# Batch 0's attention laid out by token slot, and a new order of work, in a gated attention and channel mixer kernel

## The chip, the cores and the metric

The kernel runs on one core of a Trainium2 chip. The metric is the time of one execution in device microseconds (us). The core has four engines that compute: PE (TensorE, matmuls into the banks of PSUM), DVE (VectorE), ACT (ScalarE) and POOL (GpSimd). SP (SyncE) and ACT each have a queue on which transfers are issued. Every engine works through its own instructions in order and waits on semaphores for the others.

## The reference

```python
B, H, S, D = 4, 8, 768, 48
state = zeros((B, H, D, D))
for t in range(S):
    state = alpha[:, :, t, :, None] * state + einsum('bhd,bhe->bhde', k[:, :, t], v[:, :, t])
    y[:, :, t] = einsum('bhd,bhde->bhe', q[:, :, t], state)
x = y.transpose(0, 2, 1, 3).reshape(B, S, H * D)          # 4, 768, 384
h = maximum(x.transpose(0, 2, 1) @ w_tok1, 0) @ w_tok2    # 768 -> 256 -> 768 over tokens
u = x + h.transpose(0, 2, 1)
out = u + maximum(u @ w_ch1, 0) @ w_ch2                   # 384 -> 1536 -> 384 over channels
```

Inputs and output are float32; the kernel computes its products in bfloat16.

## The kernel before, in words

**Attention blocks.** The recurrence is computed in blocks of 256 tokens: three for each of the four batches, n = 0 to 11. A block lies on 128 partitions with two neighbouring tokens on each partition (the *slots*); partitions 0 to 63 are the first 128 tokens (the first *half*) and 64 to 127 the second. For each block four loads of 384 KB bring alpha, k, q and v (`at`, `kt`, `qt`, `vt`). Blocks 0 to 2 (`WIDE`) take the logarithm of alpha for both slots (`ln`), sum it up along the tokens on PE (`cumw`), and take the exponentials of the sums and of their negatives (`E`, `IE`; `Et` for the totals of the halves). `kk` and `qq` scale keys and queries with these. Both are transposed: on PE (`trk`, `trq`) with an eviction from PSUM (`evk`, `evq`), or by a DMA transpose on SP (`dk`, `dq`, then `pq` to reorder the queries). The other blocks do the same with one sum for a pair of tokens.

`G` forms the products of keys and queries, 16 small matmuls for each half, on tiles of 48 rows by 64 columns of PE; `mask` on DVE drops the products of later keys. `K` forms the key-value product of each half, from which the state after it follows: on DVE `sa` adds the earlier state and `sm`, on DVE or POOL, multiplies with the decay. `y` adds up the masked products with v, `ia` and `ib` add the part of the earlier state, `x` copies the result from PSUM.

Before, `K` and `y` use all 128 rows of PE. For that, each half's two slots must be stacked on the 128 partitions, so copies of half a tile move them: `vs0`, `vs1` for v and `ka`, `kb`, `kc` for the keys (`vswap` and `kturn`).

**Mixer.** For each batch: `t1` (token product into 256, then `ht`), `t2` and `u` (back to tokens, plus x), the transpose of u, then 24 runs `c1` of three matmuls (L811) with a `rt` eviction each, and `c2` (L816) with the last add `o` and the store. The transpose of u goes over PE (`up`, L803, evicted by `ut`) in the batches listed in `UP`, else by two DMA transposes on SP (`ux`). The weights are loaded as float32 in 384 KB pieces (`ldw`) and cast (`cw`).

**Order.** Nothing is scheduled while the kernel is built. `build` names every operation, and `ORDER` is one long written list of these names with a letter for the engine (t PE, s ACT, v DVE, g POOL, y SP); each engine issues its own in that order, and `BUFS` lists the buffer of every value as it is first used. `f3_cumw0t` is a dummy entry: three matmuls of a zero tile with 512 columns, put before `cumw0`. DVE and POOL steps that are marked `port=True` wait for the last such step of the other engine (`shared`). In the list, batch 0's attention stands first, and the attention of a later batch is woven into the mixer of the one before.

Of the kernel before, what the change touches and what calls it, by code (L numbers as in the profile page):

```python
# [96 lines left out]
NB = 3  # L97
NX = 6
KFN = 0
LAST = (3, 0)  # L100
UP = (0, 1)
# [9 lines left out]
WIDE = (0, 1, 2)  # L111

# [3 lines left out]
def build(g):  # L116
# [8 lines left out]
    def filler(nm, bank):  # L125
        return [P.op(f"f{z}_{nm}", {"PE": pe([512] * z)["PE"], "NONE": (0.0, 0.0)}, -100, writes=[bank],
                     emit=lambda e, z=z: g.fill(bank, z)) for z in (1, 3)]

    def attention(n):
# [8 lines left out]
        def fill(nm, bank):  # L138
            return filler(f"{nm}{n}", bank) if n < NB else []

        at, kt, qt, vt = V("in"), V("in"), V("in"), V("in")
        ld = {}
        for v, nm in ((at, "at"), (kt, "kt"), (qt, "qt"), (vt, "vt")):
            ld[nm] = P.op(f"ld_{nm}{n}", {"SP": (420.0, 420.0), "ACT": (374.0, 374.0)}, -90000.0 + 10 * n, writes=[v],
                          emit=lambda e, v=v, nm=nm: g.load(e, nm, v, b, k, ld[nm]), dma=("i", IN_NS, 1500.0, 650.0))
        la, E, IE = V("la"), V("E"), V("IE")
        pkk, pkq, vb = V("pkk"), V("pkq"), V("vb")
        k_in, q_in = [ld["kt"]], [ld["qt"]]
        if n in WIDE:
            lnp = O("ln", act(800, True), 0, writes=[la], reads=[at], preds=[ld["at"]], emit=lambda e: g.lnw(la, at))  # L150
            cb = V("pair")
            cum = O("cumw", pe([384] * 4 + [4] * 8 + [16]), 2, writes=[cb, E, IE], reads=[la], preds=[lnp] + fill("cumw", cb),
                    emit=lambda e: g.cumw(cb, la))
            e1 = O("E", act(768), 4, writes=[E], reads=[cb], preds=[cum], emit=lambda e: g.exps(E, cb, 1.0))
            et = O("Et", act(16), 6, writes=[E], reads=[cb], preds=[cum], emit=lambda e: g.exptot(E, cb))
            e2 = O("IE", act(768), 3, writes=[IE], reads=[cb], preds=[cum], emit=lambda e: g.exps(IE, cb, -1.0))
        else:
# [8 lines left out]
            e1 = et = O("E", act(400), 4, writes=[E], reads=[cb], preds=[cum], emit=lambda e: g.expE(E, cb))  # L166
            e2 = O("IE", act(384), 4, writes=[IE], reads=[cb], preds=[cum], emit=lambda e: g.expIE(IE, cb))
# [5 lines left out]
        kk = O("kk", either(dve(768), pool_tt(768)), 5, writes=[pkk], reads=[kt, IE], port=True, preds=k_in + [e2],  # L173
               emit=lambda e: g.scaled(e, pkk, kt, IE, wide))
        qq = O("qq", either(dve(768), pool_tt(768)), 5, writes=[pkq], reads=[qt, E], port=True, preds=q_in + [e1],
               emit=lambda e: g.scaled(e, pkq, qt, E, wide))
# [3 lines left out]
        if n < NX:  # L180
            bk, bq = V("one"), V("one")
            trk = O("trk", pe([128] * 8), 8, writes=[bk], reads=[pkk], preds=[kk] + fill("trk", bk),
                    emit=lambda e: g.trw(bk, pkk))
            evk = O("evk", either(dve(1024, True), act(1024)), 9, writes=[tpk], reads=[bk], preds=[trk],
                    emit=lambda e: g.trwev(e, tpk, bk))
            trq = O("trq", pe([128] * 8), 8, writes=[bq], reads=[pkq], preds=[qq] + fill("trq", bq),
                    emit=lambda e: g.trw(bq, pkq))
            evq = O("evq", either(dve(1024 * 1.065), act(1024 * 1.34)), 9, writes=[tpq], reads=[bq], preds=[trq],
                    emit=lambda e: g.qev(e, tpq, g.bank(bq).bitcast(BF16)))
        else:  # L190
            evk = O("dk", {"SP": (1240.0, 1240.0)}, 9, writes=[tpk], reads=[pkk], preds=[kk],
                    emit=lambda e: g.xbar(tpk, pkk), dma=("x", 1400.0, 1180.0, 480.0))
            tqx = V("tpk")
            xq = O("dq", {"SP": (1240.0, 1240.0)}, 9, writes=[tqx], reads=[pkq], preds=[qq],
                   emit=lambda e: g.xbar(tqx, pkq), dma=("x", 1400.0, 1180.0, 480.0))
            evq = O("pq", either(dve(1024), act(1024 * 1.35, True), {"POOL": (1100.0, 1140.0)}), 9.5, port=True, writes=[tpq], reads=[tqx], preds=[xq],
                    emit=lambda e: g.qev(e, tpq, g.t(tqx)))
        gtm = V("gtm")
        masks = []
        for hf in range(2):  # L200
            gp = V("pair")
            G = O(f"G{hf}_", pe([128] * 4), 10 + hf, writes=[gp], reads=[tpk, tpq], preds=[evk, evq] + fill(f"G{hf}", gp),
                  emit=lambda e, hf=hf, gp=gp: g.gmm(gp, tpk, tpq, hf), mode="G")
            masks.append(O(f"mask{hf}_", dve(1024), 12 + hf, writes=[gtm], reads=[gp], preds=[G],
                           emit=lambda e, hf=hf, gp=gp: g.mask(gtm, gp, hf)))
        nst = 2 if k < NB - 1 else 1
        kp = V("pair")
# [4 lines left out]
        vsw = lambda hf, preds: shift(f"vs{hf}_", 10, [vb], [vt], preds, lambda e: g.vswap(e, vb, vt, hf))  # L212
        turned = n >= KFN
        if turned:
            vs = [vsw(hf, [vc]) for hf in range(2)]
            kx, kp_in = None, [kk, vc, vs[0]]
            if nst == 2:
                kx = V("kt")
                ka = shift("ka", 9, [kx], [pkk], [kk], lambda e: g.kturn(e, kx, pkk, 0))
                kb = shift("kb", 9, [kx], [pkk], [kk], lambda e: g.kturn(e, kx, pkk, 1))  # L220
                kp_in += [ka, kb, vs[1]]
            kc = shift("kc", 9, [pkk], [], [kk, trk if n < NX else evk] + ([ka] if nst == 2 else []),
# [4 lines left out]
        else:  # L227
            KO = O("K", {"PE": (276.0 if nst == 2 else 140.0, 420.0)}, 9.5, writes=[kp], reads=[pkk, vb],
                   preds=[kk, vc] + fill("K", kp) + ([prev_s[1]] if prev_s and k > 0 and n > NB else []),
                   emit=lambda e: g.kmm(kp, pkk, vb, nst), mode="G")  # L230
            vs = [vsw(hf, [KO, vc]) for hf in range(2)]
        before = prev_s if k > 0 else None
        states = [before]
        for hf in range(nst):
            s_, sp = V("ss"), states[-1]
            if sp is None:
                so = O(f"s{hf}_", dve(384), 10, writes=[s_], reads=[kp, E], preds=[KO, et],
                       emit=lambda e, s_=s_, hf=hf: g.sfirst(s_, kp, E, hf, wide, turned))
            else:
                t_ = V("tmp")  # L240
                ad = O(f"sa{hf}_", dve(384), 10 + hf, writes=[t_], reads=[kp, sp[0]], preds=[KO, sp[1]],
                       emit=lambda e, t_=t_, hf=hf, s0=sp[0]: g.sadd(t_, kp, s0, hf, turned))
                so = O(f"sm{hf}_", either(dve(384), pool_tt(384)), 11 + hf, writes=[s_], reads=[t_, E], port=True,
                       preds=[ad, et], emit=lambda e, s_=s_, t_=t_, hf=hf: g.smul(e, s_, t_, E, hf, wide))
            states.append((s_, so))
        for hf, st in enumerate(states[:2]):
            yp, x = V("one"), V("x")
            held = []
            if st:
                held.append(O(f"i{'ab'[hf]}", pe([96] * 4), 13, writes=[yp], reads=[tpq, st[0]],  # L250
                              preds=[evq, st[1]] + (fill("y", yp) if hf else []),
                              emit=lambda e, hf=hf, st=st, yp=yp: g.inter(yp, tpq, st[0], hf)))
            yo = O(f"y{hf}_", pe([48] * 8), 14, writes=[yp], reads=[gtm, vb],
                   preds=[masks[hf], vs[hf]] + held,
                   emit=lambda e, hf=hf, yp=yp, st=st: g.ymm(yp, gtm, vb, hf, not st))
            xo = O(f"x{hf}_", either(act(384), dve(384)), 16, writes=[x], reads=[yp], preds=[yo],
                   emit=lambda e, x=x, yp=yp: g.xev(e, x, yp))
            xs[(b, 2 * k + hf)] = (x, xo)
# [5 lines left out]
    def weight(nm, piece, prio, work=1100.0):  # L264
        raw = V("in")
        o = P.op(f"ldw_{nm}{piece}", {"SP": (420.0, 420.0), "ACT": (374.0, 374.0)}, prio, writes=[raw],
# [4 lines left out]
    def mixer(b):  # L271
# [44 lines left out]
        for mc in range(NDC):  # L316
            rt = V("rt")
            ro = []
            for half in range(2):
                bank = V("one")  # L320
                o = P.op(f"c1_{b}_{mc}_{half}", pe([384] * 3), m0 + (4900 + 975 * mc + 487 * half) * sc, writes=[bank],
                         reads=[ut], preds=(uts[0:2 + half] if b in UP else [uts[half]]) + [wl[("wc1", mc // 6 * 3 + p)] for p in range(3)],
# [34 lines left out]
    for b in range(B):  # L357
        mixer(b)
    return P
# [4 lines left out]
ld_at1s ld_at0y ld_qt0y ld_vt0y ld_kt0s ld_at2y f1_cumw0t ln0s f3_cumw0t f1_trk1t f1_cumw1t f1_trk0t f3_cumw1t  # L364
f1_trq0t f3_trq0t ln1s ld_qt1y f1_trq1t cumw0t cumw1t E0s ld_at3y f3_trk1t IE0s Et0s qq0v vb0s ld_kt1y kk0v trq0t E1s
f3_cumw2t vs1_0g ld_vt1y evq0v trk0t ka0s vs0_0g f1_cumw2t evk0s ld_kt3y qq1v kb0s IE1s f1_G00t G0_0t P3g ld_qt2y
f3_trq1t mask0_0v ln2s Et1s trq1t kc0g ld_vt3y K0t f1_G10t kk1v evq1s G1_0t s0_0v ld_vt2y vb1g trk1t ln13s sa1_0v
# [507 lines left out]
```

## Time and profile before

| | before |
|---|---|
| runs, median (lowest to highest) | 166.52 us (166.51 to 167.97) |
| span of the profiled execution, first to last instruction | 165.0 us |
| own time of the profiled execution | not listed beside its span; the three runs above stand for it |
| PE busy | 156.2 us, 95% of the span |
| DVE, ACT, POOL busy | 121.2, 96.2, 68.7 us |
| HBM read, written | 25.17 MB, 4.72 MB |
| granted TensorE clock | 1.000 |

The span runs from the first to the last instruction of one profiled execution; a run's time also holds what lies around it. Busy times are sums over an engine's instructions. PE's matmuls are pipelined, so that a busy PE is not one at its peak. Line numbers such as L811 are those of the kernel above.

### The profile page before, as it was taken

To read this page: it belongs to the slowest core of one execution; us is meant where nothing else is said; L and a number is where in the kernel's file an instruction comes from. 1 tells how busy PE (TensorE), PEld (TensorE's weight loads), DVE (VectorE), ACT (ScalarE), POOL (GpSimd) and SP (SyncE) were. 2 spreads that over 40 slices of the span, in tenths; PEclk is the share of its full clock that TensorE was granted. 3 is DMA by queue.
4 is the path that set the end of the run, shared out by engine and by line. 5 is a ranking of instruction groups with operands and counts; after the bars stand their busy time and mean duration, and the time that the engine had idled before them with its cause. 6 is when DMAs were issued, how large, how long until landed. Compare 5 with 4: busy or idle time off the path is not lost.

```text
span 165.0 us, 4235 instructions
## 1 busy us (share of the span) xinstructions
PE 156.2 (95%) x1683; PEld 99.2 (60%) x1683; DVE 121.2 (73%) x210; ACT 96.2 (58%) x186; POOL 68.7 (42%) x84
## 2 busy tenths in 40 slices
PE   7969769999999999999999999999999999999992
PEld 2435446666666766576666666666666656656662
DVE  4098989989898898798878999989492455524422
ACT  3599987998877837939887746913614001514110
POOL 4025659497217475792388528973300000000000
PEclk9999999999999999999999999999999999999999
DMA  4999999999999999999989996898001136200213
GB/s 121 324 325 325 337 347 316 365 327 352 371 335 347 326 315 226 307 252 264 136 198 255 211 250 120 219 181 183 0 4 48 49 75 157 105 0 0 99 72 119
DMA packets 74531, 34.48 MB, mean 209 GB/s; under 512 B 67984, under 2 KB 73488, under 8 KB 74512
## 3 DMA queue, kind: packets, MB, share of 16 engines
q1 hardware_dynamic: 50576, 23.30, 55.2%
q10 hardware_dynamic: 23936, 10.91, 24.3%
q8 instruction: 13, 0.21, 0.5%
q14 instruction: 6, 0.05, 0.1%
HBM read 25.17 MB, written 4.72 MB: 181 GB/s over the span
## 4 chain that ended last, share of the span: by engine, by line
PE 83%; DMA 4%; SPq 3%; POOL 2%; issue 2%; ACT 2%; DVE 1%; POOLq 0%; DVEq 0%
PE ps L816 29%; PE ps L811 29%; PE ps L593 14%; PE ps L792 5%; DMA in<-in_v_dram 4%; PE ps L787 4%; SPq L534 3%; PE ps L654 1%; PE ps L803 1%; POOL pkk L642 1%; DVE gtm L700 1%; POOL vb L685 1%; ACT x L684 1%; POOL ss L753 1%; ACT E L626 0%
## 5 line engine op out<-in xcount | busy, mean ns | idle before, releaser
L816 PE MATMUL ps<-wc,rt 128*128 128x384 bf16 (+1 forms) x300 | 54.7, 320 | 0.0
L811 PE MATMUL ps<-ut,wc 128*128 128x384 bf16 x288 | 51.3, 326 | 0.0
L782 ACT ACTIVATE rt<-ps 128x384 bf16<-128x384 f32 x54 | 24.4, 490 | 35.4 <-PE ps L811 34.7
L811 PEld LDWEIGHTS <-wc 128*128 128x128 bf16 x288 | 27.1, 98 | 16.7
L816 PEld LDWEIGHTS <-rt 128*128 128x128 bf16 x300 | 27.5, 98 | 15.9
L700 DVE TENSOR_TENSOR gtm<-ps,mk 128x1024 bf16<-128x1024 f32 x24 | 28.7, 1219 | 4.8 <-PE ps L593 3.4
L784 DVE TENSOR_SCALAR rt<-ps 128x384 bf16<-128x384 f32 x42 | 21.7, 551 | 9.2 <-PE ps L811 9.2
L820 DVE TENSOR_TENSOR o<-ps,u 128x384 f32<-128x384 f32 (+1 forms) x25 | 13.1, 537 | 10.0 <-PE ps L816 9.1
L685 POOL CAST vb<-in 64x384 bf16<-64x384 f32 (+1 forms) x18 | 10.9, 608 | 15.2 <-DVE pkk L642 8.9
L593 PE MATMUL ps<-zs 128*128 128x512 bf16 x38 | 12.7, 452 | 2.9 <-DVE zs L496 1.1
L684 ACT CAST x<-ps 128x384 bf16<-128x384 f32 x17 | 7.8, 477 | 10.7 <-PE ps L593 10.5
L796 DVE TENSOR_TENSOR u<-ps,x 128x384 bf16<-128x384 f32 x24 | 11.8, 550 | 3.0 <-PE ps L792 3.0
L642 DVE TENSOR_TENSOR pkq<-in,E 128x768 bf16<-128x768 f32 x8 | 7.6, 954 | 5.4 <-ACT E L626 5.2
L787 PE MATMUL ps<-x,wt 128*128 128x384 bf16 x48 | 11.1, 325 | 0.5 <-DVE gtm L700 0.4
L684 ACT CAST vb<-in 64x384 bf16<-64x384 f32 (+1 forms) x18 | 11.1, 618 | 0.7 <-DMA in<-in_v_dram 0.2
L642 POOL TENSOR_TENSOR pkk<-in,IE 128x768 bf16<-128x768 f32 x5 | 9.1, 1816 | 4.9 <-DVE pkk L685 3.2
L753 POOL TENSOR_TENSOR ss<-tmp,E 128x384 bf16<-128x384 f32 x11 | 9.2, 833 | 3.2 <-DVE tmp L750 2.9
L750 DVE TENSOR_TENSOR tmp<-ps,ss 128x384 f32<-128x384 f32 x16 | 8.8, 552 | 1.0 <-PE ps L593 0.5
L792 PE MATMUL ps<-ht,wt 128*128 128x384 bf16 x48 | 9.5, 326 | 0.0
L593 PEld LDWEIGHTS <-gtm 128*128 128x128 bf16 x192 | 7.4, 96 | 2.7 <-DVE gtm L700 0.9
L593 PEld LDWEIGHTS <-tpk 48*64 48x64 bf16 x384 | 6.1, 106 | 4.9 <-issue 4.3
L593 PE MATMUL ps<-vb,gtm 128*128 128x48 bf16 x192 | 8.6, 183 | 0.4 <-DVE gtm L700 0.4
(91 smaller groups left out, 216.6 us busy)
## 6 DMA issues: line engine op xcount, KB each, us to landing
in<-in_moe_w_ch_dram SPq DMA_DIRECT2D x10, 384.0 KB, 6.2
in<-in_alpha_dram SPq DMA_DIRECT2D x9, 384.0 KB, 6.8
out_dram<-o SPq DMA_DIRECT2D x16, 192.0 KB, 2.5
in<-in_q_dram SPq DMA_DIRECT2D x7, 384.0 KB, 6.3
in<-in_v_dram ACTq DMA_DIRECT2D x7, 384.0 KB, 6.0
in<-in_k_dram ACTq DMA_DIRECT2D x6, 384.0 KB, 5.7
in<-in_k_dram SPq DMA_DIRECT2D x6, 384.0 KB, 6.2
in<-in_v_dram SPq DMA_DIRECT2D x5, 384.0 KB, 7.2
```

The source lines that it names most:

```text
L593: return self.pe.matmul(out, lhsT=lhsT, rhs=rhs, start=start, stop=stop, skip_group_check=True)
L642: self.shared(self.eng[e].tensor_tensor(self.t(dst)[:, :, :, 0:D], self.t(src).rearrange("p h s d -> p s h d"), bass.AP(tensor=f.tensor, o ...
L684: return self.act.copy(d, s)
L685: return self.shared(self.eng[e].tensor_copy(d, s))
L700: self.nc.vector.tensor_tensor(self.t(gtm)[:, hf, :, :], self.pair(gp).rearrange("p a (j t) -> p (a j) t", t=128), bass.AP(tensor=m.tensor ...
L782: self.act.activation(d, s, AF.Relu)
L784: self.nc.vector.tensor_scalar_max(d, s, 0.0)
L787: self.pe.matmul(self.bank(bank)[:, 0:HD], lhsT=self.wt1[:, kc, m * 128 : m * 128 + 128], rhs=self.t(x), start=(kc == 0), stop=(kc == NS - 1))
L792: self.pe.matmul(self.bank(bank)[:, 0:HD], lhsT=self.wt2[:, kc, i * 128 : i * 128 + 128], rhs=self.t(hts[kc]), start=(kc == 0), stop=(kc = ...
L811: self.pe.matmul(self.bank(bank)[:, 0:HD], lhsT=self.wc1[:, kc, mc * 128 : mc * 128 + 128], rhs=self.t(ut)[:, 3 * half : 3 * half + 3, kc, ...
L816: self.pe.matmul(self.bank(bank)[:, 0 : cz - ca], lhsT=self.t(rts[mc][0])[:, i * 128 : i * 128 + 128], rhs=self.wc2[:, mc, ca:cz], start=( ...
L820: self.nc.vector.tensor_tensor(self.t(o)[:, ca:cz], self.bank(bank)[:, 0 : cz - ca], self.t(u)[:, i % 3, ca:cz], ALU.add)
```

## The change

- Blocks 0 to 2 keep the slots as they are: `G` is split by slot instead of by half (`gslot`, with the new mask table `mkw`), and `K` and `y` run on tiles of 64 rows, one for each half, both halves in one run (`khalf`, `yslot`). The half-tile copies of these blocks are gone. The earlier state is added on PE with an identity matmul (`kadd`, named `A`), and one DVE product with the decay (`sfirst`) makes the new state.
- `Et` is joined to `E`: the totals lie behind the sums in both banks.
- Block 5's keys and batch 1's u are transposed by DMA instead of on PE (`KX`, `QX`, `UP`).
- All loads are issued on SP. The stores are on both queues: 19 on ACT and 6 on SP, where it was 8 and 17.
- The first half of `w_ch1` is loaded in thirds of its columns, each with all its rows, so that a third serves two of the twelve column blocks.
- `ORDER` and `BUFS` are new throughout. The dummy matmuls are 28 instead of 38, and all stand in batch 0's attention.

```diff
-NX = 6
+KX = (5, 6, 7, 8, 9, 10, 11)
+QX = (6, 7, 8, 9, 10, 11)
-UP = (0, 1)
+UP = (0,)
+LOADQ = ({"SP": (420.0, 420.0)}, {"SP": (420.0, 420.0)})
...
+        if wide:
+            kps = [V("one") for _ in range(nst)]
+            K = O("K", {"PE": (350.0, 530.0)}, 9.5, writes=kps, reads=[pkk, vb], preds=kk + [vc],
+                  emit=lambda e, first=before is None: g.khalf(kps, pkk, vb, first), mode="Y")
+            for hf in range(nst):
+                kp, s_, sp = kps[hf], V("ss"), states[-1]
+                KO = K
+                if sp is not None:
+                    KO = O(f"A{hf}_", pe([384]), 9.6 + hf, writes=[kp], reads=[sp[0]], preds=[K, sp[1]],
+                           emit=lambda e, kp=kp, s0=sp[0]: g.kadd(kp, s0))
+                so = O(f"s{hf}_", dve(384), 10 + hf, writes=[s_], reads=[kp, E], preds=[KO, et],
+                       emit=lambda e, s_=s_, kp=kp, hf=hf: g.sfirst(s_, kp, E, hf, wide))
+                states.append((s_, so))
...
+    def gslot(self, gp, tpk, tpq, sl):
+        tk, tq = self.t(tpk), self.t(tpq)
+        for j in range(4):
+            for hf in range(2):
+                for r in range(2):
+                    pr = slice(r * 64, r * 64 + D)
+                    self.mm(self.bank(gp, r)[hf * 64 : hf * 64 + 64, j * 128 : j * 128 + 128],
+                            tk[pr, (sl * 4 + j) * 128 + hf * 64 : (sl * 4 + j) * 128 + hf * 64 + 64],
+                            tq[pr, j * 256 + hf * 128 : j * 256 + hf * 128 + 128], True, True)
+
+    def maskslot(self, gtm, gp, sl):
+        m = self.mkw[:, 1 - sl : 129 - sl]
...
+    def khalf(self, kps, pkk, vb, first):
+        kk, vv = self.t(pkk), self.t(vb)
+        for j in range(4):
+            for sl in range(2):
+                for hf, kp in enumerate(kps):
+                    ph = slice(hf * 64, hf * 64 + 64)
+                    self.mm(self.bank(kp)[:, 96 * j : 96 * j + 96], kk[ph, sl, 2 * j : 2 * j + 2, :],
+                            vv[ph, sl, 2 * j : 2 * j + 2, :], j == 0 and sl == 0, (first and hf == 0) and sl == 1)
+
+    def kadd(self, kp, s0):
+        self.mm(self.bank(kp)[:, 0:HD], self.idn, self.t(s0), False, True)
+
+    def yslot(self, yps, gtm, vb, first):
+        gg, vv = self.t(gtm), self.t(vb)
+        for h in range(H):
+            for sl in range(2):
+                for hf in range(2):
+                    ph = slice(hf * 64, hf * 64 + 64)
+                    self.mm(self.bank(yps[hf])[:, h * D : h * D + D], gg[ph, sl, 4 * (h % 2) + h // 2, :],
+                            vv[ph, sl, h, :], first[hf] and h == 0 and sl == 0, h == H - 1 and sl == 1)
...
 ORDER = """
+ld_at0y ln0s f8_cumw0t f1_cumw0t cumw0t IE0s ld_at1y ln1s ld_kt0y kk0g ld_qt0y E0s qq0v ld_vt0y ld_qt1y vb0v ld_at2y
+ld_kt1y f6_cumw1t f1_cumw1t cumw1t E1s ld_at3y trk0t qq1v evk0v IE1s ld_vt1y ld_at4y ld_kt2y kk1g ln2s ld_qt2y ld_kt3y
+ld_vt2y P3g f1_trq0t trq0t evq0s K0t s0_0v ldw_wt10y ld_vt3y ln13s ld_qt3y f4_cumw2t f1_cumw2t cumw2t vb1g ldw_wt11y
+G1_0t E2s mask1_0v A1_0t ldw_wt20y ldw_wt21y ld_at5y ldw_wc13y r13s ldw_wc15y ldw_wc14y ld_kt4y s1_0v G0_0t trq1t
...
+t2_1_0t o_0_5v ld_kt7y u_1_0v c2_0_4_2t t2_1_2t u_1_2v t2_1_3t t2_1_1t u_1_1v t2_1_4t vs0_6s u_1_4v u_1_3v P7g
+c2_0_0_0t lnP7s st_0_5s c2_0_4_3t ka6g ld_at8y ln18s P8g o_0_4v c2_0_2_2t kb6s c2_0_2_3t st_0_4s o_0_2v t2_1_5t dk6y
+c2_0_0_1t u_1_5v cum7t kc6s k0a7v c2_0_0_2t ld_qt7y vs1_6s K6t c2_0_0_3t IE7s kk7v lnP8s cum8t E7s ux_1_0y c1_1_3_0t
...
```

399 lines of the change are left out of this document (212 added, 187 removed), and 22 rows, old and new, of the table BUFS.

## The prediction

> **What bounds the kernel now.** I read the windows first, cut where the chain of waits changes its kind, then the chain itself, then who waited for whom.
>
> ```profile
> 0.00:31.39 31.39, 25.74 (x339) 15.16 (x340) 22.98 (x44) 24.49 (x41) 14.88 (x29) 1.00 1.04 305
> 31.39:37.34 5.95, 5.95 (x90) 4.29 (x90) 5.34 (x11) 5.56 (x10) 5.66 (x7) 1.00 1.10 338
> 37.34:162.00 124.66, 124.55 (x1257) 79.74 (x1254) 92.54 (x156) 66.12 (x137) 48.14 (x49) 1.00 0.73 180
> ```
>
> First number after the window: its length; then PE, weight loads, DVE, ACT, POOL busy. From 31.39 us on PE never waits. Before, it is idle for 31.39 - 25.74 = 5.65 us, and much of its busy time there is the dummy matmuls (38 of 512 columns). So time can come from two places only: an earlier end of the head (batch 0's attention, first token matmuls), or less PE work after it.
>
> ```profile
> 14.06 7.23 DMA in<-in_v_dram
> ...
> 23.31 1.83 POOL pkk L642
> ...
> 31.39 0.86 PE ps L787 x4
> ...
> 32.99 2.06 PE ps L792 x12
> 35.05 0.17 PE ps L593 x4
> 35.22 0.77 PE ps L803 x12
> 35.99 1.07 PE ps L593 x38
> 37.06 0.44 PE ps L803 x6
> 37.51 2.48 PE ps L811 x15
> ```
>
> The chain in order of time (start, length, what). The head hangs on loads until 21.29, then on batch 0's third block, then PE alone counts. L811, the first channel matmul, begins at 37.34: the milestone of my sum. After it come 124.66 us of PE and 3.0 us of last add and store.
>
> **The sum's base.** The profiled span is 165.0; the runs have a median of 166.52. No own time of the profiled run is given, so I take 1.5 us to lie around the span.
>
> **The head, part by part.** (1) All loads on SP. From 8 to 16 us ACT issued one load, and the core still moved 325 to 327 GB/s, so one queue suffices: 384 KB at 325 GB/s is 1.21 us. The two first alphas share the engines and are used at 5.00; alone, the first lands at about 3.8, the n-th at 3.8 + 1.21(n - 1). Position gives: vt2 (15th) 20.7, wc14 (25th) 32.8. Check: the page's first eight slices hold 25.8 loads' bytes by 33 us. Before, the cast of vt2 began at 23.65. 24 load issues of about 0.38 us leave ACT; 19 instead of 8 stores come to it, off the path where PE never waits. A second mask table costs DVE a fill and four small copies at the start, where it waits 5.19 us for the first E.
>
> (2) Token slots. For three blocks, 13 half-tile copies (0.50 to 0.51 each, 6.6 us of ACT, POOL, DVE) and three small exponentials (0.18) go. Four state steps change from add plus product (0.56 + 0.83 on DVE and POOL) to a 384-column identity matmul (0.16) and one DVE product (0.55): 0.68 less on the chain each time. PE gets: cumulative sums three 16-column matmuls more; key-value products 40 on 64-row tiles for 20 (8 of 96 columns took 0.34; the new runs lie between 0.35, side by side, and 0.68); y 32 for 16 per block. Eight y take 0.20 in the chain, so 32 cost between 0.32 (two tiles at once) and 0.80 (25 ns each); I take 0.45, nearest the 16 G tiles (0.35, 22 ns each). At the dear end PE has 1.6 us more, covered by the 5.65 idle; without that cover it would be paid.
>
> Row first: after a G run on tiles the next three L811 take 0.59 instead of 0.49, so changing tiles costs 0.10. The Trainium skill, TensorEngine Tiling (Array Packing), Tiling Modes, speaks against this change: switching the mode drains TensorE. Six runs more are 0.6 us by it, in the head beside waits; the sum is the same by row and rule.
>
> (3) Dummy matmuls: 28 for 38. The first eleven come every 0.43 us until 5.7, later ones at 0.21, so nine end at 4.9, and the first cumulative sum, begun at 4.9 instead of 6.6, runs partly slow (+0.6). Its input is there at 4.6.
>
> (4) The head walked by hand in the new order, each engine in its own sequence, durations from the rows of before, some 0.05 for each hand-over. Block 0: ln 3.8 to 4.6, sums on PE to 6.1, then ACT does IE, the ln of block 1 and E (0.81 each) to 8.6; kk takes 1.82 on POOL from 7.1 to 8.9, and only then qq 0.96 on DVE to 9.9, since DVE and POOL take turns at the steps marked as sharing a port. ACT is now the long engine: E and IE of block 1, ln of block 2 and block 0's query eviction (1.30) end at 13.1. Block 1: kk waits for its load and ends at 14.4; ACT ends the key eviction at 17.7. Block 2: after a mask (1.22) and a state (0.55) of the earlier blocks DVE does kk and qq from 18.6 to 20.5; ACT evicts the queries to 22.6; after G, DVE has a mask, a state and a mask, to 26.5; y and the x copies end at 28.0. The last token-1 matmul ends at 28.7, ht at 29.9. For the second token product wt21 (21st, 28.0) must be cast too: POOL ends that at 29.6. DVE has four steps of batch 1's first block in between and does the six u of 0.55 from 30.5 to 33.8 (before: 33.49 to 36.37); ut 0.55 to 34.4. The 25th load, 32.8, plus a 0.82 cast behind two other POOL steps gives 34.6. So L811 begins at **34.6**, 2.75 earlier. Bounds: not before 32.8 + 0.6 = 33.4 (gain 3.9); gain 0 if chains slip. The loads already stand right behind the attention: that is what is late next.
>
> **PE work after the milestone.** Batch 1's 18 transposes of u leave PE (0.67 + 0.34 in the chain), and block 5's eight of k (0.45); one inter product of 0.17 moves behind. Net -1.3 us. Four evictions go with them. Their work becomes three DMA transposes on SP (ut row: 1.28 each). On SP ux waits behind dk6 and the load of qt7, and behind it stand dq6 and the loads of block 8.
>
> ```profile
> L668 SPq DMA_TRANSPOSE ut<-u x4: 1242/1280/1307, 104.3 to 136.7; - x4
> DMA to landing us min/median/max: 3.2/3.2/3.9
> ```
>
> These are the transposes of u for batches 2 and 3 (ns of the issue; us to landing). In the new order batch 1 has between the third u's matmul and the first L811 seven c2 runs of 0.49, two t2 of 0.33, two cumulative sums and one K: 4.8 us of PE. Less about 1.0 for u on DVE, 3.8 stand against 3.2 to 3.9. For batches 2 and 3 the same count gives 3.75 and 3.9, less 0.75: 3.0 and 3.15. I allow **1.2 us** of new PE waits; from nothing to 6.6, the longest wait of an SP transpose before:
>
> ```profile
> SPq L664 <- POOL in L578: 6.6, 1, 6.6
> ```
>
> On the same queue dk5, new, waits for POOL's kk of block 5, and behind it stand vt5, at6 and three wc2 pieces; these are wanted after 24 c1 runs (11.7 us), so a hold of a few us is covered; beyond that it would be paid in full.
>
> The wc1 weights in thirds of columns change nothing: wc12 (27th, lands 35.3) is needed after eight c1 runs, 34.6 + 3.9; wc11 (30th, 38.9) after thirteen, 41. Without that lead each late piece would cost 1.21.
>
> The end of the last batch has the same final half add and store, but two 192 KB stores just ahead: 0 to 0.5, I take 0.1.
>
> **Sum.** -2.75 (head) - 1.3 (PE work) + 1.2 (waits) + 0.1 = -2.75. 166.52 - 2.75 = **163.8**; its own range: 166.52 - 3.9 - 1.3 = 161.3 to 164.8.
>
> **Rivals.**
> A: the head does not move. For it: ACT and DVE are busy 24.49 and 22.98 of 31.39 us, so an in-order slip of any chain delays all, and six state, mask and u steps stay. Against: vt2 comes 3 us sooner, 6.6 us of copies go. Then -1.3 + 1.2 + 0.1: 166.5.
> B: slower. SP's single queue is the place: in batch 1 a transpose or load ahead of ux waits as the 6.6 us row did. Waiting t beyond the spare 0.0 to 0.6 us stops PE for t, since everything behind is L811 of the same batch. 6.6 replaces the 1.2: 166.52 - 2.75 - 1.2 + 6.6 = 169.2. It decides the sign from t = 4.0. For: 64 loads, 19 transposes and 6 stores in one line, and one 384 KB load issue took up to 2.98 us under back-pressure. Against: the wait list of PE after 31.4 us is empty with sixteen transposes already on SP; 64 loads need 77 us of the some 100 until the last block.
> C: the new order fits fully: no new waits and L811 held by the loads alone: 161.3.
> D: the slots do not do what they say: K and y run one tile after the other at the dear end and no cover is left in the head: 163.8 + 1.6 = 165.4.
>
> **Chances.** Forecast 0.50; C 0.13; A 0.13; B 0.13; D 0.11. A measurement of this kernel can tell about 1% (1.7 us; the runs span 1.46) from no change. Faster by over 1%, below 164.85: forecast and C, and a fourth of A and D together, 0.69; within 1%: the rest of A and D, 0.18; slower: 0.13. The range 161.0 to 168.0 leaves out most of B (0.11) and the best of C (0.05). The likeliest case's own is 161.3 to 164.8.
>
> **What would show it.** First L811 near 34.6, the first ln begun at 3.8 instead of 5.00, no half-tile copies in the first 25 us; the PE idle after the milestone 1 to 1.5 us and released by DMA ut; PE's work after the milestone near 123.3. Wrong: L811 later than 36, or a single PE wait over 3 us on ut or on a load.

## The result and the profile after

The change makes the kernel slower: 172.07 us (median of four runs, 170.97 to 173.1) against 166.6 us, a ratio of 1.030 with an interval from 1.024 to 1.037. The forecast was 163.8 us, and its range ended at 168.0. The profiled execution took 173.1 us, with a span of 171.4. The mean granted clock of the four executions was 0.98, 0.99, 1.00 and 0.986 (at 173.1, 172.5, 170.97 and 171.65 us): stretches of 3.4 us at half clock, told below, are part of the loss, but the execution at full clock is still 4.4 us above 166.6. Medians here are of all executions of a version, while a ratio and its interval leave out those that took over 1.5% longer than the fastest of their kernel, and set the others against the executions of the kernel before that were on record by then (4 to 19, with medians of 166.6 to 167.25 us).

The windows of the changed kernel, cut where its head ends (columns as before; the first channel matmul, now L890, first runs at 36.43, and without a break from 36.88):

```profile
0.00:31.00 31.00, 26.46 (x406) 16.41 (x407) 19.51 (x44) 20.91 (x30) 15.01 (x25) 0.94 1.01 283
31.00:36.88 5.88, 5.67 (x87) 3.82 (x86) 5.75 (x12) 5.41 (x10) 3.48 (x4) 1.00 1.09 366
36.88:168.04 131.16, 124.92 (x1231) 78.69 (x1231) 87.31 (x145) 69.81 (x141) 52.24 (x53) 0.99 0.76 182
```

Three things differ from the rows of before. The head ends 0.5 to 0.9 us earlier, not 2.75. After it PE is idle for 131.16 - 124.92 = 6.24 us, where it never waited. And the last-but-two column, the granted clock of PE, is 0.94 and 0.99 where it was 1.00. Who stops PE after the head, and what stops DVE (waits: us in total, times, longest):

```profile
PE ps L646 <- DVE u L875: 2.6, 1, 2.6
PE ps L646 <- DVE o L899: 2.3, 2, 2.1
PE ps L646 <- DMA tpk<-pkk: 1.3, 2, 1.0
...
DVE o L899 <- DMA out_dram<-o: 6.6, 4, 2.8
```

The first three rows make up the 6.2 us. No row names `ut`, the releaser that the forecast had named. The row to read is the last: the final add `o` (L899) waits for *stores* of earlier `o` tiles. The chain shows how this reaches PE (start, length, what):

```profile
67.29 4.52 DMA out_dram<-o
...
71.94 0.10 DVE o L899
...
72.41 0.56 DVE u L875
...
73.11 0.33 PE ps L646 x4
```

`o` has three buffers. The new order puts four last adds of batch 0 within 8 us (64.2 to 71.9), but the written list `BUFS` gives them two buffers only: o_0_1 and o_0_4 the first, o_0_5 and o_0_2 the second. So the fourth add, o_0_2, waits 2.78 us for the store of o_0_5, while the third buffer is not in use. That store landed 4.5 us after its issue, and it was issued 2.05 us after its add had ended (65.24), because ACT first stood waiting for POOL:

```profile
67.23 0.52 ACT L637 ACTIVATE la<-in 128x384 bf16<-128x384 f32 x1 [1.51 <-POOL in L631]
67.29 0.34 ACTq L627 DMA_DIRECT2D out_dram<-o  x1
```

u_1_5 stands behind o_0_2 in DVE's line, and PE's K6 stands behind u_1_5, for whose bank it waits. PE's stop of 2.1 us at 97.98 is of the same kind: o_1_2 waits for the first buffer, into which o_0_3 was added by 79.4 and whose store ACT issued only at 92.97; the third buffer had been free since its store landed at 87.2. In the kernel before, stores landed as late (3.5 to 5.4 us), but its list of waits has no such row. What follows the first stop is a second loss (PE alone: length, busy time, granted clock, DMA share, GB/s):

```profile
70.19:73.60 3.41, 0.84 (x11) 1.00 1.23 214
73.60:77.00 3.40, 3.40 (x17) 0.50 1.27 147
```

After a stretch of 3.41 us in which PE worked 0.84, the next 3.41 us run at half clock: 1.7 us of work lost. A like pair stands in the head: 2.03 us busy of 3.41 up to 25.80, then half clock to 29.21. The Trainium skill, TensorE: Matmul & The Clock Gate, Part 1, says that the clock falls to half after an idle window of about 3.4 us. The length agrees; the trace shows that the window need not be wholly idle. Nor does the busy time alone decide: the two half-clock stretches begin 47.8 us apart, 14 times 3.41, and in another stretch of this spacing, 94.09 to 97.50, PE was busy for 1.79 us only and the clock stayed full to 100.9.

The profiled span, against the forecast's own sum (span about 162.3):

| | forecast | measured | difference |
|---|---|---|---|
| end of the head (L890 without a break) | 34.6 | 36.88 | +2.3 |
| PE work after it, at full clock | 123.3 | 124.92 - 1.7 = 123.2 | 0 |
| PE idle after it | 0.1 + 1.2 | 6.24 | +4.9 |
| half clock after the head | 0 | 1.7 | +1.7 |
| last add and store | 3.1 | 3.4 | +0.3 |

### The profile page after: what moved, and what is told of

It reads as the page before. It is cut to its first block, busy times and chain, and to the rows that moved or that the text cites. A ratio compares the mean times of both kernels' runs of the same rounds, so it can differ in the third digit from the quotient of the medians.

```text
span 171.4 us, 4289 instructions
## 1 busy us (share of the span) xinstructions
PE 157.0 (92%) x1722; PEld 98.9 (58%) x1722; DVE 112.9 (66%) x200; ACT 96.1 (56%) x179; POOL 70.7 (41%) x82
## 4 chain that ended last, share of the span: by engine, by line
PE 56%; DMA 21%; SPq 7%; POOL 6%; DVE 4%; issue 3%; ACT 1%; DVEq 0%; POOLq 0%
PE ps L890 24%; PE ps L895 18%; PE ps L646 9%; DMA in<-in_q_dram 7%; DMA in<-in_moe_w_ch_dram 5%; DMA tpk<-pkk 4%; SPq L581 4%; DMA in<-in_alpha_dram 3%; DMA out_dram<-o 3%; PE ps L866 2%; DVE u L875 2%; PE ps L712 1%; POOL in L692 1%; PE ps L871 1%; POOL in L696 1%
## 5 line engine op out<-in xcount | busy, mean ns | idle before, releaser
L890 PE MATMUL ps<-ut,wc 128*128 128x384 bf16 x288 | 53.3, 332 | 0.2
L890 PEld LDWEIGHTS <-wc 128*128 128x128 bf16 x288 | 27.1, 99 | 18.0 <-issue 1.4
L863 DVE TENSOR_SCALAR rt<-ps 128x384 bf16<-128x384 f32 x39 | 20.5, 549 | 9.9 <-PE ps L890 8.8
L758 DVE TENSOR_TENSOR gtm<-ps,mk 128x1024 bf16<-128x1024 f32 x18 | 21.4, 1217 | 4.0 <-PE ps L646 2.4
L899 DVE TENSOR_TENSOR o<-ps,u 128x384 f32<-128x384 f32 (+1 forms) x25 | 13.2, 537 | 15.9 <-PE ps L895 8.2
L700 POOL TENSOR_TENSOR pkk<-in,IE 128x768 bf16<-128x768 f32 x9 | 16.4, 1817 | 11.2 <-ACT IE L687 4.4
L646 PE MATMUL ps<-tpq,tpk 48*64 48x128 bf16 x384 | 8.1, 219 | 3.9 <-DVE o L899 2.1
L646 PE MATMUL ps<-rt 128*128 128x512 bf16 x28 | 9.3, 460 | 1.1 <-DVE rt L538 1.1
L832 POOL TENSOR_TENSOR ss<-tmp,E 128x384 bf16<-128x384 f32 x8 | 6.7, 833 | 8.0 <-DVE tmp L829 5.2
L692 POOL TENSOR_TENSOR in<-in,in 128x384 f32<-128x384 f32 x6 | 6.0, 994 | 7.3 <-DVE gtm L774 3.4
L743 POOL CAST vb<-in 64x384 bf16<-64x384 f32 (+1 forms) x11 | 6.8, 619 | 4.9 <-DVE ss L832 4.2
L696 POOL TENSOR_TENSOR in<-in,lf 128x384 f32<-128x384 f32 x6 | 6.0, 999 | 6.6 <-DVE pkk L700 5.7
```

Source lines behind the costliest of these rows:

```text
L646: return self.pe.matmul(out, lhsT=lhsT, rhs=rhs, start=start, stop=stop, skip_group_check=True)
L700: self.shared(self.eng[e].tensor_tensor(self.t(dst)[:, :, h0:h1, 0:D], self.t(src)[:, h0:h1].rearrange("p h s d -> p s h d"), bass.AP(tens ...
L758: self.nc.vector.tensor_tensor(self.t(gtm)[:, hf, :, :], self.pair(gp).rearrange("p a (j t) -> p (a j) t", t=128), bass.AP(tensor=m.tensor ...
L863: self.nc.vector.tensor_scalar_max(d, s, 0.0)
L890: self.pe.matmul(self.bank(bank)[:, 0:HD], lhsT=self.wc1[:, kc, mc * 128 : mc * 128 + 128], rhs=self.t(ut)[:, 3 * half : 3 * half + 3, kc, ...
L899: self.nc.vector.tensor_tensor(self.t(o)[:, ca:cz], self.bank(bank)[:, 0 : cz - ca], self.t(u)[:, i % 3, ca:cz], ALU.add)
```

## The experiments

Where numbers of buffers change, every class named gets its buffers anew, the one that has been free longest first; line numbers shift with each edit. Each version has one profiled execution. In the eight whose loads up to there are the same (the change itself, 1, 2, 6, 9, 10, 11 and 13) the head ends, without a break, between 36.09 and 37.50 us, and the last piece of w_ch1 that it needs begins its cast between 35.25 and 36.37, so a difference of less than 1 us between two heads says little.

**1. Room for the stores** (`o` six buffers).

```diff
-    "rt": 20, "o": 3,
+    "rt": 17, "o": 6,
```

> The changed kernel with six buffers for the last add (o) instead of three; to make room rt has 17 instead of 20. Theory one (each store lands 4 to 5 us after its issue while loads run, four last adds come within 8 us, so DVE's o waits for a buffer, the u behind it comes late and PE waits for a bank): the DVE waits on stores (6.6 us in four) fall under 0.5, the PE waits of 2.6 and 2.1 us go, and with the first the half-speed window at 73.6 us; 172.1 falls by 4.5 to 6.5, to 165.6 to 167.6. Theory two (SP's one line of loads, transposes and stores makes the transposes late): the PE waits only change their releaser to tpk or ut, and the time stays above 170.5.

Measured: 169.34 us, ratio 1.015 (1.011 to 1.019). DVE's row for `out_dram<-o` falls from 6.6 to 0.4 us, and the half clock after the head is gone; PE's idle time there falls from 6.24 to 4.02 us. That mends 2.7 us, half of the loss, and less than the 4.5 to 6.5 of theory one. The edit changes two things, the number of `o` buffers and which add gets which: it shows what the waits for stores cost, and not that three buffers are too few. No run keeps three and uses the third. The waits that are left:

```profile
PE ps L658 <- POOL tpq L755: 1.6, 2, 1.2
PE ps L902 <- DMA ut<-u: 1.4, 2, 1.0
PE ps L902 <- DVE rt L875: 0.7, 1, 0.7
```

**2. Eight dummy matmuls in the head's idle places.**

```diff
-G0_2t        -K2t        -t1_0_1_0t
+g1_G0_2t G0_2t   +g3_K2t K2t   +g4_t1_0_1_0t t1_0_1_0t
```

> The changed kernel with eight more dummy matmuls (1.7 us) at three places between 22 and 26 us where PE waits in the head: one before the first G of block 2, three before its K, four before the first t1. Theory one (the half-speed window of 25.8 to 29.2 us follows from PE's idle time before it, and holds up the head's end): no half-speed window in the head, first L811 1 to 1.7 us earlier than 36.9, time 0.8 to 1.7 us lower. Theory two (the head's end is set by the landing of the last wc1 piece at 35.95): the window goes, but L811 still begins at 36.6 to 37.0 and the time stays within 0.6 us.

Measured: 171.28 us, 1.027 (1.020 to 1.033). No half clock in the head any more (a stretch came at 94.9 us instead, after 1.23 us of work in 3.41). The head ends at 36.09 without a break instead of 36.88, 0.8 us earlier, and the time falls by as much, between the two theories; the last piece of w_ch1 is cast from 35.25 instead of 36.00. The store waits are all there (6.5 us on DVE).

**3. The slots alone, first try**: the order, queues and pieces of w_ch1 of before, batch 0's attention by slots.

```diff
-KX = (5, 6, 7, 8, 9, 10, 11); UP = (0,); ORDER: new
+KX = (6, 7, 8, 9, 10, 11);    UP = (0, 1); ORDER: of before, with the slots' steps
```

> The kernel before with batch 0 by token slot alone: its order, queues, w_ch1 pieces and PE transposes, with the half-tile copies, Et and the second product of the state left out of the list, the two y of a block as one run at the place of the later one. Theory one (the slots shorten the head): first L811 0.3 to 1.0 us before 37.34, time 165.6 to 166.3. Theory two (tile changes and doubled small matmuls cost as much): 166.6 to 167.3. In either, not the 172.1 of the whole change.

Measured: 170.78 us, 1.026 (1.021 to 1.031), the first channel matmul at 42.7. No theory had that. It is confounded: I had given one product a bank in which it waited for a mask (1.6 us), and the head had two stretches at half clock.

**4. The loads alone**: the kernel before, its 24 loads on ACT issued on SP instead.

```diff
-ld_at1s ld_kt0s ... ld_vt10s
+ld_at1y ld_kt0y ... ld_vt10y
```

> The kernel before with its 24 ACT loads issued on SP at the same places of the list, nothing else. Theory one (one queue carries all loads as fast; the prediction's step): 166.6, within 0.8. Theory two (a load that waits for its buffer holds every later load, transpose and store): loads land later, PE waits appear after 31 us, 168 to 171.

Measured: 169.65 us, 1.012 (1.007 to 1.016). This is theory two. The head is no worse (37.0, with 300 GB/s over its first 37 us against 309), so the forecast's reading that one queue feeds the DMA engines holds; but a line in order lets a load that waits for its buffer hold all behind it. In the profiled execution, one of the longer ones (170.66 us):

```profile
SPq L534 <- DVE wc L685: 3.4, 1, 3.4
```

```profile
PE ps L816 <- ACT wc L684: 2.3, 1, 2.3
```

The first row is SP: a load of v waits for a buffer until DVE has cast the piece of w_ch2 in it, and behind it in the line stands the load of another piece of w_ch2. The second is PE, waiting for that piece. A stretch at half clock follows (62.4 us), and these 2.3 and 1.7 us are the whole difference of the spans (169.0 against 165.0). The Trainium skill, DMA: Bandwidth & Descriptors, Issuing engines are not separate DMA queues, says that issuing on several engines saves only issue time. By bandwidth the trace agrees; the loss comes from what waits behind a waiting load. That the other executions, 1.2% above the kernel before, lose at the same place is likely, but they have no profile.

**5. More load buffers** for the changed kernel.

```diff
-    "in": 19, "rt": 20,
+    "in": 22, "rt": 14,
```

> The changed kernel with 22 load buffers (in) for its 19, paid for with 14 rt buffers for its 20; o stays at 3, order and queues are as they are. Theory one (waits for load buffers in SP's single line hold the head): SP's waits in the first 31 us for a load buffer to come free (1.5 us for the buffer of vb2, and the 1 to 3 us behind POOL and ACT) go, wc14 lands at 33 to 34.8 instead of 35.95, the first channel matmul starts at 34.0 to 35.8 instead of 36.4, and the time falls by 1 to 2.5 us from the changed kernel's 172.1, to 169.6 to 171.1; the o stores' waits (6.6 us on VectorE) stay. Theory two (the rate of the loads themselves sets the head): wc14 lands within 0.5 us of 35.95 and the time stays at 171.5 to 172.5.

Measured: 171.25 us, 1.022 (1.014 to 1.030). The chain of the head:

```profile
27.40 7.54 DMA in<-in_moe_w_ch_dram
...
34.98 0.84 POOL wc L755
...
35.87 2.94 PE ps L902 x17
```

wc14 lands 1.0 us earlier than in the changed kernel (34.94 against 35.95), and the head ends at 35.87 instead of 36.88. Both lie just below the spread of the eight heads told above, so SP's waits for buffers cost something, between 0.2 and 1.6 us at the end of the head; the time falls by 0.8.

**6. Edits 1 and 2 together.**

> The two earlier edits together: 6 o buffers (17 rt), and 8 dummy matmuls ahead of the head's idle places (one before G0_2, three before K2, four before t1_0_1_0). Theory one (the two losses are separate and add up): -2.7 us for the store waits and -0.8 to -1.7 us for the half-speed window in the head, so 167.6 to 168.8. Theory two (the loads set the end of the head, and the half-speed window there lies under the loads' time): the same as with 6 o buffers alone, 169.0 to 169.8.

Measured: 168.83 us, 1.011 (1.006 to 1.016), with 11, which cannot be told from it, the best version of the change that computes the whole result. Its mean granted clock is 0.997. Compare the row after the head with those of before and after:

```profile
36.87:163.88 127.01, 123.42 (x1232) 78.52 (x1232) 87.74 (x145) 70.23 (x141) 52.40 (x54) 1.00 0.76 189
```

PE works 1.1 us less than before (124.55), and is idle 3.6 us.

**7. The slots alone, second try**: as 3, with y1 right after ia1, y0 in a free bank, and twelve dummy matmuls ahead of trq2, ia1, trk3, ia2 and K2.

> Before's order, queues, w_ch1 pieces and TensorE transposes, with batch 0's attention by slots alone, as in the run of slots alone before, but y1 placed right after ia1, y0 in bank 3 so that no product waits for a bank, and 12 dummy matmuls in the gaps the smaller work leaves. Theory one (the slots themselves save time, and what was lost was the stale order): the first channel matmul starts no later than 37.4, there is no half-speed window in the head, and the time is 165.5 to 167.0. Theory two (the slots cost as they stand: less work on TensorE, the same chain through VectorE and ScalarE, loads that end at the same time): the first channel matmul starts at 37.4 to 40 and the time is 167 to 169.5. Above that: the slots' smaller tiles have a cost of their own that I have not named.

Measured: 170.01 us, 1.018 (1.012 to 1.023), above both theories. The clock is full throughout, and after the head PE is idle 0.05 us, as before. All of the loss lies in the head, which ends at 40.9:

```profile
40.90:165.48 124.58, 124.53 (x1257) 79.74 (x1254) 92.39 (x156) 66.08 (x137) 48.24 (x49) 1.00 0.70 175
```

```profile
27.25 3.58 PE ps L661 x69
...
30.86 0.56 DVE ss L840
31.42 1.14 DVE gtm L789
...
32.60 0.65 PE ps L881 x3
```

The chain runs PE (of whose 3.58 us six dummy matmuls take 1.47), a state on DVE, then the two masks of block 2 one after the other on DVE (31.34 to 33.68), for which PE waits. Without the half-tile copies, this head is 3.5 us longer. So in an order made for halves the slots bring nothing; whatever the new kernel's head gains, it gains together with its order.

**8. Buffers, dummy matmuls and vt7 earlier** (five `o`, 21 `in`, 14 `rt`).

```diff
-ld_kt7y ... ld_qt7y ... dq7y ... ld_vt7y dk8y
+ld_kt7y ... ld_qt7y ld_vt7y ... dq7y ... dk8y
```

> The changed kernel with 5 o buffers, 21 load buffers, 14 rt buffers, the 8 dummy matmuls of the head, and the load of vt7 moved up in SP's line from behind the transposes of dq7 to right behind qt7. Theory one (the order of buffers and of SP's line is what was wrong, not the slots): 166 to 168, at or a little above the kernel before; a head that ends at 34.5 to 36, no wait of o for a store over 0.5 us, and the chain no longer through vt7 at 80 us. Theory two (the single line of loads costs by itself, wherever a buffer waits): 168.3 to 169.8.

Measured: 172.09 us, 1.027 (1.018 to 1.037): as slow as the change itself, and neither theory. PE has a new wait behind the head:

```profile
PE ps L911 <- DMA ut<-u: 3.2, 1, 3.2
```

The first transpose of u of batch 1 is issued at 65.90, 1.8 us behind the load of vt7, and lands 7.7 us later, where the two of the changed kernel took 4.9 and 5.9. A stretch at half clock follows at 72.9. Why the transpose took so long is not shown; that it shared the engines with vt7 would fit.

**9 and 10. Loads back on ACT**: 17 loads, in the changed kernel (9) and in the version of experiment 6 (10), at their places in the order.

```diff
-ld_at7y ld_vt7y ld_qt6y ... ld_vt10y ldw_wc24y ldw_wc25y
+ld_at7s ld_vt7s ld_qt6s ... ld_vt10s ldw_wc24s ldw_wc25s
```

> The changed kernel with 17 of its loads (the ones of batches 1 to 3 that the kernel before issues on ScalarE, and two pieces of w_ch2) moved from SP's line to ScalarE's, at their places in the order; nothing else. Theory one (the single line of loads is a loss of its own, apart from the store waits): after the head no wait of TensorE for a load or a transpose of more than 1 us in batch 1, and 1 to 2.5 us less than the changed kernel's 172.1, so 169.6 to 171.1. Theory two (the line costs nothing by itself; only what waits for o and the half-speed windows count): 171.6 to 172.6, or more, since ScalarE issues 17 loads of 0.4 to 0.9 us.

> The run with 6 o buffers and the 8 dummy matmuls (168.8 us) with the same 17 loads on ScalarE's line. Theory one (the rest of the loss, 3.5 us of TensorE waits in batches 1 and 2, comes from loads behind waiting transposes in SP's line): the chain no longer passes through vt7 at 79.8 us, those waits fall below 1.5 us, and the time is 166.0 to 167.4, level with the kernel before. Theory two (the waits come from the order on VectorE and GpSimd, and the loads are just late in it): 168.3 to 169.3.

Measured: 177.46 us, 1.050 (1.040 to 1.061), and 173.05 us, 1.034 (1.026 to 1.041). My theory fell: by the ratios, two lines of loads are worse by about 2% in this order, some 3.4 and 3.8 us. The clock in 10 is full. Two waits of 10 after the head, ACT's and SP's:

```profile
ACT rt L879 <- PE ps L908: 7.7, 8, 1.9
...
SPq L740 <- POOL pkq L718: 10.1, 3, 7.3
```

ACT reaches each load only when its evictions are done, and they wait for PE, as long as in version 6 (7.4 us) but now with loads behind them; and SP, no longer held by its loads, stands at the transposes, once for 7.3 us. The chain still passes vt7, now landing at 86.8 instead of 84.7. That the places in the list were right for one engine only is my reading of this; no run moves the loads to better places on ACT.

**11. The transposes of u on ACT** (version 6).

```diff
-ux_1_0y ux_1_1y ux_2_0y ux_2_1y
+ux_1_0s ux_1_1s ux_2_0s ux_2_1s
```

> The same run (6 o buffers, 8 dummy matmuls, 168.8 us) with the loads left on SP's line and the four transposes of u of batches 1 and 2 (ux) on ScalarE's. Theory one (ux is late because it stands behind waiting loads and transposes in SP's line): the 1.0 us wait for ut goes, loads behind ux come 1 to 2 us earlier, and the time is 167.6 to 168.5. Theory two (ux waits for u itself, or the path lies elsewhere): 168.6 to 169.4.

Measured: 169.29 us, 1.009 (1.004 to 1.014): no difference from version 6, and the wait for `ut` stays (1.0 us there, 0.9 here). What stands in SP's line ahead of `ux` does not hold it: in version 6 SP itself waits there for u.

```profile
SPq L744 <- DVE u L893: 3.3, 2, 2.2
```

**12. All of it**: six `o`, 21 `in`, 13 `rt`, dummy matmuls, and the 17 loads on ACT.

> 6 o buffers, 21 load buffers, 13 rt buffers, the 8 dummy matmuls, and the 17 loads on ScalarE's line: the changed kernel with each known loss mended. Theory one (the slots save what I summed, some 1.3 us of TensorE's work and up to 1 us of the head, once nothing waits): 165.0 to 166.3, faster than the kernel before. Theory two (13 rt buffers or the order bring waits of their own, and the head has no more to give): 166.7 to 168.5.

Measured: 175.22 us, 1.051 (1.043 to 1.060). Neither theory. It is 1.7% slower than 10, so the numbers of buffers (21 `in`, 13 `rt`, dealt out anew) cost as well as the loads on ACT; which of them does is not separated.

**13. vt7 right ahead of dk7** (version 6).

```diff
-ld_at9y ... dk7y ... dq7y ... ld_vt7y dk8y
+ld_at9y ld_vt7y ... dk7y ... dq7y ... dk8y
```

> The run with 6 o buffers and the 8 dummy matmuls (168.8 us), with the load of vt7 moved in SP's line from behind the transposes dk7 and dq7 to right ahead of dk7. Theory one (what is left of the loss in batch 1 is the place of vt7 in the order: GpSimd's cast of it at 84.8 us holds all that is queued behind it): that cast starts at 80 to 82, the 1.1 us wait for tpq at 106 goes, and the time is 167.0 to 168.2. Theory two (the three waits come from the batch's order on VectorE and GpSimd as a whole; another wait takes the place): 168.4 to 169.4.

Measured: 171.59 us, 1.024 (1.019 to 1.030). The wait for `tpq` shrinks to 0.4, and another takes its place. The same wait of PE in version 6, and then here:

```profile
PE ps L908 <- DVE rt L881: 1.4, 1, 1.4
```

```profile
PE ps L911 <- DVE rt L884: 3.1, 1, 3.1
```

What SP waited for between 70 and 86 us tells why:

```profile
SPq L602 <- POOL pkq L721: 2.6, 1, 2.6
```

The moved load keeps the buffer that the list gave it, and this buffer comes free only when a query step on POOL is done. So vt7 issues at 77.90, 1.9 us before its old time (79.81), and dk7, now behind it, at 78.32 instead of 75.06; the transposed keys land at 82.7, the steps of block 7 follow, and `rt` stands behind them on DVE. Here, as in experiment 8, moving one entry of the list moved the loss.

**14. One load fewer ahead of wc14** (version 6).

```diff
-ld_at5y ldw_wc13y ... ldw_wc15y ldw_wc14y
+ldw_wc13y ... ldw_wc15y ldw_wc14y ld_at5y
```

> The run with 6 o buffers and the 8 dummy matmuls with the load of at5 (not used before the first channel matmul) moved in SP's line from ahead of the last three pieces of w_ch1 to right behind them: one load of 1.2 us fewer ahead of wc14. Theory one (the loads' rate, with the 16 DMA engines busy for the whole head, sets the end of the head): wc14 lands 0.8 to 1.4 us earlier than without the edit, the first channel matmul starts at 35.4 to 36.2 instead of 36.87, and the time is 167.6 to 168.4. Theory two (the chain through TensorE, ScalarE and the up-transposes sets it, as in the profile of the run without the edit): wc14 lands earlier, but the first channel matmul stays within 0.4 us of 36.87, and the time at 168.5 to 169.2.

Measured: 170.82 us, 1.023 (1.018 to 1.028), and my premise was false: at5's logarithm feeds a cumulative sum that stands ahead of the first channel matmul in PE's line.

```profile
26.75 8.27 DMA in<-in_alpha_dram
...
36.12 0.53 ACT la L658
...
36.70 0.43 PE ps L667 x6
```

The alpha load lands at 35.02; POOL's product and ACT's logarithm follow, PE waits 2.0 us for them, and then runs at half clock.

**15. Moves 13 and 14 together.**

> Both moves, vt7 ahead of dk7 and at5 behind wc14, on the run with 6 o buffers and the 8 dummy matmuls. Theory one (both count and add up): 166.2 to 167.6, level with the kernel before. Theory two (neither counts): 168.4 to 169.4.

Measured: 173.49 us, 1.036 (1.029 to 1.042): both losses are there.

**16 to 18. Fewer bytes, nothing moved**: in the changed kernel (16), the kernel before (17) and version 6 (18), wt20, wt21 and wc13 are fetched in their first eighth, 1 MB less.

```diff
-dma(t, self.w[1][128 * piece : 128 * piece + 128, :])
+dma(t[:, 0:96], self.w[1][128 * piece : 128 * piece + 128, 0:96])
```

> The changed kernel, with the two pieces of w_tok2 and one piece of w_ch1 (wt20, wt21, wc13: 384 KB each) fetched only in their first eighth, which the cast repeats eight times, so part of the weights is left out: 1 MB, or about 3.2 us at 325 GB/s, less to fetch ahead of wc14; every instruction stays. Theory one (the rate of the loads sets the end of the head, so the work that the slots save on VectorE and ScalarE has nothing to shorten): wc14 lands at 32.5 to 34 instead of 35.95, the first channel matmul starts at 34.0 to 35.4 instead of 36.4, and the time falls by 1 to 2.4 us, to 169.7 to 171.1. Theory two (the chain through the engines sets it): wc14 lands earlier and the first channel matmul stays at 36.0 to 36.9, the time within 0.6 us of 172.1.

> The kernel before with the same bytes left out (wt20, wt21, wc13 in their first eighth, repeated by the cast; part of the weights is left out). Theory one (before, the chain through VectorE, GpSimd, ScalarE and the transposes sets the end of the head, as its chain of waits shows): the first channel matmul stays at 36.8 to 37.5 and the time within 0.6 us of 166.8. Theory two (the loads set the head of the kernel before too): it starts 1 us or more earlier and the time falls by 1 to 2.5 us.

> The run with 6 o buffers and the 8 dummy matmuls (168.8 us, head ends at 36.87) with the same bytes left out (part of the weights is left out). Theory one (loads): the head ends at 34.3 to 35.6 and the time is 166.3 to 167.8. Theory two (the chain through TensorE, ScalarE and the up-transposes, which ends at the same time there): 36.3 to 36.9, and 168.3 to 169.0.

The chain at the end of the head, 16 first, then 17:

```profile
30.52 0.83 POOL wt L751
...
34.91 0.57 DVE ut L751
...
35.53 3.10 PE ps L898 x18
```

```profile
37.46 2.48 PE ps L819 x15
```

The kernel before does not move: first channel matmul at 37.3, ratio 1.003 (1.000 to 1.006). In the changed kernel it starts at 35.5 (36.43, steady 36.88, without the edit), and from 14 us on the chain has no load in it and ends in casts and `ut`; the time is 170.5 us (172.07), a ratio of 1.018 (1.010 to 1.026). Version 18: head 35.65 instead of 36.87, 167.93 us instead of 168.83, ratio 1.0065 (1.003 to 1.010). Both heads end below all eight told above (36.09 to 37.50, 36.7 on average). So in the changed kernel the loads hold the head by about 1 us, and before they hold it by nothing; the gain is less than theory one's 34.0 to 35.4, since the engines' chain ends right behind. The row after the head of 18:

```profile
35.65:162.12 126.47, 123.79 (x1232) 78.69 (x1232) 87.86 (x145) 70.40 (x141) 51.22 (x52) 1.00 0.75 187
```

Even so PE is idle 2.7 us in it, a little more than the head (1.7) and the PE work (0.8) gain together.

## Why the prediction was wrong, point by point

**PE work after the head**: right in kind, a little large. Forecast 1.3 us less; the versions at full clock there show 0.8 to 1.1 less (123.42 to 123.79 against 124.55), the changed kernel itself, with 1.7 taken off for the half clock, 123.2.

**New waits of PE, +1.2**: the step that failed. It measured 6.24 us, and 1.7 at half clock behind it. The term that was put at nothing is the stores: they come to ACT, says the forecast, "off the path where PE never waits". Behind them PE stopped for 2.6 and 2.3 us. I looked for the releaser on SP, at `ux`; in the changed kernel `ut` never stopped PE. Once the waits for stores are gone it does, for 1.4 us (version 1) and 1.0 (version 6), close to the 1.2 that I allowed, so that the allowance was fair for `ut` and stores were left out of it. I counted their issues and not what waits for their landing: the next add that the list gives the same buffer of `o`. The rows for it were there: o_0_1, o_0_5, o_0_4 and o_0_2 stand close together with two buffers between them, st_0_5 stands on ACT behind a step that needs POOL, and stores of the kernel before took 3.5 to 5.4 us to land. Experiment 1 brought 2.7 us back, which shows this half of the loss. The sign given beforehand held for the head (later than 36: 36.43, steadily from 36.88), and not for the waits: none of PE's was over 3 us, and none on `ut` or a load.

**The head, -2.75**: right in kind, too large. It came to 0.5 to 0.9. The walk gave the engines' chain 34.6, and 16 and 18 put it at 35.5 to 35.65 once bytes are out of the way, a gain of 1.7 to 1.8. Ahead of that stand the loads: wc14 was to land at 32.8 and landed at 35.95. The formula of 1.21 us for each load takes a line that never stops. SP did stop, for buffers (1.5 us for the one that vb2 frees, and others), and the rate fell to 211 GB/s from 18 to 20 us and to 217 from 24 to 26. By the bytes this is some 0.9 us of the lateness, and three more buffers brought wc14 forward by 1.0. The other 2.2 us are bytes of other loads: wc14 is the 25th load issued, but when it landed at 35.95 the loads' queue had moved 10.55 MB, which is 26.8 loads of 384 KB, since four more had been issued behind it (28.69 to 33.02) and moved beside it. By the formula 26.8 loads end at 35.0. The formula counts as if each load landed before the next began.

**Dummy matmuls**: I asked only whether the first sum would run slow. The half clock came at 25.8, in gaps of the attention, and in the lee of the store wait. In the head it costs some 0.8 us: without the eight dummy matmuls the head ends at 36.88, 37.25 and 37.50 (the change, 1 and 9), with them at 36.09 to 36.87 (2, 6, 10, 11 and 13); from version 1 to version 6 the time falls by 0.5.

**Small matmuls**: in the changed kernel 32 of y took 0.51 us to the start of what follows (forecast 0.45, bounds 0.32 to 0.80), 16 of K 0.45 and 0.53 (0.35 to 0.68). Rival D falls.

**Rivals.** B had the sign, with a probability of 0.13, and named SP's line; that line costs the kernel before 1.2% (experiment 4), but not by way of `ux`, and in the new order two lines are worse still. A comes close for the head alone.

**What stays open.** Version 6 keeps 3.6 us of idle time in batches 1 and 2, in three waits. Each attempt at one of them (8, 10, 12, 13) made a wait longer. That the order as a whole is the cause, and no single entry, is what this suggests; no run shows it. Whether the list of buffers alone, with the third `o` buffer used, mends what experiment 1 mended is open too. No version beats the kernel before.

## What to carry to other kernels

Count a store twice: its wait in the line that issues it, and its landing. Its buffer is held through both: for o_0_5 2.05 and 4.5 us, for o_0_3 13.6 and 4.4. When an order brings producers of one buffer class together, ask for each when the buffer that it is given comes free, and whether another one is free by then. And an order written for one distribution of steps or queues is part of the price of changing either: the slots in an order made for halves made the head 3.5 us longer here, and the same loads on another engine cost some 3.4 to 3.8 us.

## What the runs showed of the hardware

PE fell to half clock after a stretch of 3.41 us in which it had been busy 2.03 us, and not after one in which it had been busy 1.79; I had expected a stretch without work, and what decides is open. One stop of 2.6 us thus cost 4.3. Loads issued behind another one moved 1.8 loads' bytes before it had landed. And taking 1 MB of 11 out of a head in which the DMA engines' mean share is 1.02 (changed) or 1.05 (before) moved its end by about 1 us in the changed kernel and by nothing in the kernel before: such a share does not say that the loads set the end.
